# A written TensorE order for the second attention of a four-layer decode kernel

## Chip, cores and metric

The kernel runs on one core of one Trainium2 chip. The metric is the device time of one execution in microseconds. The time before is the median of five runs, 185.16 us (183.58 to 186.29). The profiled execution is a further run.

## The reference

Two kinds of layer alternate, attention and GLU, each used twice with the same weights and the same K and V caches:

```python
x = x + _A_ref(_layernorm(x), A_k_cache, A_v_cache, A_wq, A_wo)   # attention 0
x = x + _B_ref(_layernorm(x), B_w_gate, B_w_up, B_w_down)         # GLU 0
x = x + _A_ref(_layernorm(x), A_k_cache, A_v_cache, A_wq, A_wo)   # attention 2
x = x + _B_ref(_layernorm(x), B_w_gate, B_w_up, B_w_down)         # GLU 1
# _A_ref: q = x @ wq; softmax(q k^T / sqrt(128)) v over the last 2048 positions; @ wo
# _B_ref: (sigmoid(x @ w_gate) * (x @ w_up)) @ w_down
```

The batch is 4, one new position each, D = 512, 32 query heads on 8 KV heads of 128, F = 1792, all in bf16.

## The kernel before

Both attentions walk over the 8 KV heads; one head (all four batches) is a unit, named 0.0 to 0.7 in the first attention and 2.0 to 2.7 in the second. The second takes the heads in reverse, 7 down to 0. A unit consists of: q spread to block form (`qx` on TensorE, L706, and its copy `qe` on ScalarE, L711), the scores S (4 mask matmuls L733 and 16 score matmuls L740), the maximum over them (DVE, L748 to L760), exp (ScalarE, L763), P permuted on TensorE (`pp`, L772), copied (L774) and transposed by DVE into `ebuf` (L779), P times V (PV), the sums of P and their reciprocal, and WO, the product with that head's rows of wo, summed over all units.

In the first attention DVE also transposes K in place (L718), so the second one finds it ready in SBUF. The second attention uses a wide form of PV (`pv_wide`, L897: 16 matmuls of 512 columns) for units 2.0 to 2.6: the product is transposed (`tv`, L905), reduced (`rd`, L910), shifted, added and scaled (`sh`, `ad`, `av`, L912 to L917) on DVE, turned back by two small matmuls (`tr`, L927), copied (`oc`, L933) and multiplied by wo in rows (`wo_wide`, L946). After unit 2.7's PV, which has the narrow form (L817), `wo_back` (L957, L963) brings the row sums of the seven units into the column form that unit 2.7's WO (L977) adds to. Then come the addition to x, the layer norm, the gate and up projections of GLU 1 (L1053), hT (L1080), x as rows (`xrow`, L1096), and the down projection (L1111).

SBUF holds an arena of 50 slots; 32 hold K, the rest is a pool of tiles of two slots, 1 MB each. All large loads go through SP's queue in one fixed order (L391). A load is given the tile that was released first by the time it is planned, and waits for the last reader of that tile. The order of releases in the program text thus decides which work a load waits for. In the second attention 14 V loads follow the four wq loads; one V tile was kept in SBUF and another one is parked in PSUM ("stash") and brought back by four DVE transposes (L510). Tiles are freed by the parts of q (`q_proj`, L671), by S (its head's K is not needed again), by PV and by WO. Small working buffers of the wide form lie in one of the K tiles of unit 2.0 (`wide_buffers`).

The order on each compute engine comes from a list scheduler, `_schedule` (L86): it keeps an estimate of when each operation could start, from durations in `_TM` (L263), and picks the earliest program place among those startable within a tolerance. SP alone follows program order. Semaphores follow from the dependencies. What `attn` (L986) writes down is: units two ahead in S (`front`), then PV, then `turn` for P two ahead, then WO.

Of the kernel before, what the change touches and what calls it, by code (L numbers as in the profile page):

```python
# [40 lines left out]
class _Plan:  # L41
    def __init__(self):
        self.ops = []
        self.last_w = {}
        self.readers = {}
        self.bank_eng = {}
        self.bank_cur = {}
        self.bank_prev = {}

    def op(self, eng, name, dur, emit, r=(), w=(), banks=(), dma_bytes=0, dma_rate=0.0, after=(), lazy=0.0):  # L50
# [26 lines left out]
        for t in w:  # L77
            self.last_w[t] = o
            self.readers[t] = []
        deps.discard(o)  # L80
# [168 lines left out]
class _SlotPool:  # L249
# [17 lines left out]
    pe_pair=34.0, pe_small=230.0, pe_f32=450.0, pe_row=85.0, pe_sq=300.0,  # L267
# [5 lines left out]
def build(nc, A_x, A_k, A_v, A_wq, A_wo, B_wg, B_wu, B_wd, out, cfg=None):  # L273
# [7 lines left out]
    assert GROUPS == [[0, 1, 2, 3]]  # L281
    N_DMA_SEMS = cfg.get("N_DMA_SEMS", 24)
# [32 lines left out]
    with es:  # L315
# [343 lines left out]
        def q_proj(k, b0, b1, variance):  # L659
            assert b0 == 0 and b1 == NB  # L660
            after = ()
            for n, i in enumerate((0, 1) if k == 0 else (1, 0)):
                qb = OBS[n]
                for c in range(NC):
                    name, o = wq_part(k, c, i)
                    s = need(name)

                    def e_q(pe, c=c, s=s, qb=qb, o=o):
                        last = None
                        for hh in range(4):  # L670
                            last = pe.matmul(ps[32 * hh:32 * hh + NB, qb, :], xn[:, c * NB:(c + 1) * NB],  # L671
                                             tile_ap(s)[:, o + hh * 512:o + (hh + 1) * 512],
                                             start=(c == 0), stop=(c == NC - 1))
                        return last
                    P.op("tensor", "q%d_%d_%d" % (k, i, c), 4 * tm["pe_row"], e_q,
                         r=tok(s) + [("xn",)], w=[("qrow", i)], banks=(qb,), after=after if k else ())
                    done(name)
                if variance is not None:
                    variance()
                    variance = None  # L680
                P.op("vector", "qt%d_%d" % (k, i), c_dve(512),
                     lambda v, qb=qb: v.transpose(  # L682
                         ebuf[:, :], ps[:, qb, :].rearrange("p (x k t) -> p x t k", k=32, t=2)),
                     r=[("qrow", i)], w=[("e", 0), ("e", 1)], banks=(qb,))
                qi = qh[:, i * 64:(i + 1) * 64]
                qc = P.op("vector", "qc%d_%d" % (k, i), c_dve(64),
                     lambda v, qi=qi: v.tensor_tensor(
                         qi.rearrange("p (c b r) -> p c b r", c=4, b=NB),
                         ebuf[:, :].rearrange("p (r c y) -> p c y r", c=4, y=32)[:, :, 0:NB],
                         lnr[:, 0:NB].unsqueeze(1).unsqueeze(3).broadcast_to([128, 4, NB, REP]), ALU.mult),  # L690
                     r=[("e", 0), ("e", 1), ("lnr", 0)], w=[("qh", i)])
                if k and n == 0:
                    fresh.append(qc)
                    after = (qc,)
# [28 lines left out]
        def softmax_unit(tag, hk):  # L723
# [3 lines left out]
            bank, pt = (OBS[0], 2) if u == HKV else (SB[k2], k2)  # L727
            q_unit(tag, hk, k2)

            def e_s(pe):  # L730
# [4 lines left out]
                for cp in range(4):  # L735
# [10 lines left out]
            mk = mxt[:, k2 * 32:(k2 + 1) * 32]  # L746
            P.op("vector", "mx" + tag, c_dve(512),
                 lambda v: v.tensor_reduce(nmax[:, k2:k2 + 1], ps[:, bank, :], AXX, ALU.max),  # L748
                 r=[("pss", pt)], w=[("mx", k2)], banks=(bank,))
            for g in range(2):  # L750
                P.op("vector", "nx%d%s" % (g, tag), tm["dve_small"],
                     lambda v, g=g: v.tensor_copy(nmax[64 * g:64 * g + 64, 4 + k2:5 + k2],  # L752
                                                  nmax[64 - 64 * g:128 - 64 * g, k2:k2 + 1]),
                     r=[("mx", k2)], w=[("nx", k2, g)])
            P.op("vector", "mk" + tag, tm["dve_small"],
                 lambda v: v.scalar_tensor_tensor(mk, nmax[:, 4 + k2:5 + k2].broadcast_to([128, 32]), nmax[:, k2:k2 + 1],
                                                  maskr[:, :], ALU.max, ALU.add),
                 r=[("mx", k2), ("nx", k2, 0), ("nx", k2, 1), ("maskr",)], w=[("mk", k2)])
            P.op("vector", "nm" + tag, tm["dve_small"],
                 lambda v: v.tensor_reduce(nmax[:, 2 + k2:3 + k2], mk, AXX, ALU.max, negate=True, apply_transpose=True),  # L760
                 r=[("mk", k2)], w=[("nm", k2)])
            P.op("scalar", "ex" + tag, c_act(512) + 200.0,
                 lambda a: a.activation(prow[:, :].rearrange("p (m x t) -> p m x t", x=32, t=2),  # L763
                                        ps[:, bank, :].rearrange("p (m t x) -> p m x t", x=32, t=2), ACTF.Exp, bias=nmax[:, 2 + k2:3 + k2], scale=1.0,
                                        accum_out=psm[:, k2:k2 + 1]),
                 r=[("pss", pt)] + [("nm", k2)], w=[("prow",), ("psm", k2)], banks=(bank,))
            return k2

        def turn_p(tag, k2, pb, wide=False):
            ob = OBS[k2]  # L770
# [10 lines left out]
            if wide:  # L781
                sums(tag, k2)
                return
# [22 lines left out]
        def pv_unit(tag, h, k2, tiles):  # L806
            ob = OBS[k2]
            ev = ebuf[:, k2 * 256:(k2 + 1) * 256].bitcast(BF16).rearrange("p (m x t) -> p t m x", x=32, t=2)
            for bp, name in tiles:
# [58 lines left out]
        def sums(tag, k2):  # L868
# [4 lines left out]
            out_ = ps[0:64, WB, k2 * 8:k2 * 8 + 8]  # L873
            P.op("tensor", "sb" + tag, tm["pe_f32"],
                 lambda pe: pe.matmul(out_, rest["mb"], pr, start=True, stop=True),
                 r=[("pr", k2), ("mb",)], w=[("psb", k2)], banks=(WB,))
            P.op("vector", "ri" + tag, c_dve(8) + 60.0, lambda v: v.reciprocal(rv[0:64, :], out_),
                 r=[("psb", k2)], w=[("rinv", k2)], banks=(WB,))
            P.op("vector", "rm" + tag, c_dve(64),
# [5 lines left out]
        def pv_wide(tag, h, k2, tiles):  # L885
# [22 lines left out]
            def e_rd(v):  # L908
# [5 lines left out]
            P.op("vector", "ad" + tag, c_dve(32), lambda v: v.tensor_tensor(o32[0:64, :], o32[0:64, :], osh[0:64, :], ALU.add),  # L914
                 r=[("o32", k2), ("osh", k2)], w=[("o32", k2)])
            P.op("vector", "av" + tag, c_dve(256),
# [4 lines left out]
                 r=[("o32", k2), ("rm", k2)], w=[("av", k2)])  # L921
            q0 = 16 + k2 * 16

            def e_tr(pe):
                last = None
                for bb in range(2):
                    last = pe.matmul(ps[:, WB, q0 + bb * 8:q0 + bb * 8 + 8], av[0:64, bb * 128:(bb + 1) * 128], selm[0:64, :],  # L927
                                     start=True, stop=True)
                return last
            P.op("tensor", "tr" + tag, 2 * tm["pe_pair"], e_tr, r=[("av", k2), ("selm",)], w=[("pst", k2)], banks=(WB,))  # L930
            op = opb[:, k2 * NR:(k2 + 1) * NR]
            P.op("vector", "oc" + tag, c_dve(16),
                 lambda v: v.tensor_copy(op.rearrange("p (m b i) -> p i m b", b=2, i=2),  # L933
                                         ps[:, WB, q0:q0 + 16].rearrange("p (i m b) -> p i m b", i=2, b=2)),
                 r=[("pst", k2)], w=[("opb", k2)], banks=(WB,))
# [16 lines left out]

        def wo_back():
            halves = (ebuf[:, 0:256], prow[:, :].bitcast(F32))
            for n, tk in enumerate(("e", "prow")):
                P.op("scalar", "wr%d" % n, c_act(256),
                     lambda a, n=n: a.copy(halves[n], ps[:, PBS[1], n * 256:(n + 1) * 256]),  # L957
                     r=[("psr",)], w=[(tk, 0) if n == 0 else (tk,)], banks=(PBS[1],))

            def e_b(pe):  # L960
                last = None
                for c in range(NC):
                    last = pe.matmul(ps[:, WB, c * NR:c * NR + NB], halves[c // 2][:, c % 2 * 128:(c % 2 + 1) * 128],  # L963
                                     selw[:, :], start=(c == 0), stop=False, skip_group_check=True)
                return last
            P.op("tensor", "wr", NC * tm["pe_f32"], e_b, r=[("e", 0), ("prow",), ("selw",)], w=[("psw",)], banks=(WB,))
# [19 lines left out]
        def attn(L):  # L986
            hs = list(range(HKV)) if L == 0 else list(range(HKV))[::-1]

            def front(ui):
                h = hs[ui]  # L990
                if L == 0:
                    k_transpose(h)
                k2 = softmax_unit("%d.%d" % (L, ui), h)
                if L == 2:
                    if ui == 0:
                        wide_buffers(4 * h + 2, [o for o in P.ops if o.name == "S2.0"][0])
# [15 lines left out]
            for ui, h in enumerate(hs):  # L1012
# [7 lines left out]
                if ui + 2 < HKV:  # L1020
                    turn(ui + 2)
# [235 lines left out]
```

## Time and profile before

| | |
|---|---|
| median of five runs | 185.16 us |
| profiled execution: its own time, its span | 184.38 us, 182.7 us |
| bytes moved, mean rate over the span | 72.07 MB, 395 GB/s |
| DVE busy | 106.4 us, 58% |
| PE busy (matmuls) | 103.3 us, 57% |
| ACT, POOL busy | 32.1 us, 13.2 us |
| second attention, first q matmul to last WO matmul | 121.2 to 171.5 us |

In the 40 slices of the page each stands for 4.6 us; a digit is the busy share in tenths. The chain of waits follows the end of the program back to what released each step; "SPq" in it is time in which SP was issuing a transfer. In tables of stretches each engine has its busy time and its number of instructions, then the granted TensorE clock, the DMA engines' busy share and GB/s. A time to landing runs from the issue of a transfer to the point at which all 16 DMA engines have reported their part.

### The profile page before, as it was taken

To read this page: it belongs to the slowest core of one execution; us is meant where nothing else is said; L and a number is where in the kernel's file an instruction comes from. 1 tells how busy PE (TensorE), PEld (TensorE's weight loads), DVE (VectorE), ACT (ScalarE), POOL (GpSimd) and SP (SyncE) were. 2 spreads that over 40 slices of the span, in tenths; PEclk is the share of its full clock that TensorE was granted. 3 is DMA by queue.
4 is the path that set the end of the run, shared out by engine and by line. 5 is a ranking of instruction groups with operands and counts; after the bars stand their busy time and mean duration, and the time that the engine had idled before them with its cause. 6 is when DMAs were issued, how large, how long until landed. Compare 5 with 4: busy or idle time off the path is not lost.

```text
span 182.7 us, 3750 instructions
## 1 busy us (share of the span) xinstructions
PE 103.3 (57%) x1588; PEld 54.8 (30%) x1599; DVE 106.4 (58%) x280; ACT 32.1 (18%) x80; POOL 13.2 (7%) x65
## 2 busy tenths in 40 slices
PE   1434425572817408254186566436968769756794
PEld 1002111342413405214146531312323324325632
DVE  6209997659394393744942633212898997945250
ACT  2002032121120202102002001001064333322010
POOL 7000010110010100101001000000001000010000
PEclk9999999999999999999999999999999996968559
DMA  5999999999999999999999999999999999999970
GB/s 200 422 425 423 425 414 419 420 422 420 414 422 418 420 420 416 420 422 425 405 425 414 409 402 417 374 386 383 400 335 423 429 420 420 427 406 406 410 315 12
DMA packets 12305, 72.07 MB, mean 395 GB/s; under 512 B 1145, under 2 KB 1153, under 8 KB 5633
## 3 DMA queue, kind: packets, MB, share of 16 engines
q1 hardware_dynamic: 12280, 71.84, 96.3%
q8 instruction: 12, 0.20, 0.4%
q14 instruction: 5, 0.03, 0.0%
q10 hardware_dynamic: 8, 0.00, 0.0%
HBM read 71.83 MB, written 0.00 MB: 393 GB/s over the span
## 4 chain that ended last, share of the span: by engine, by line
DMA 44%; DVE 22%; PE 17%; SPq 10%; issue 3%; ACT 3%; POOL 0%; ACTq 0%
DMA arena<-in_A_v_cache_dram 23%; DMA arena<-in_B_w_down_dram 11%; SPq L391 10%; DVE arena L718 9%; PE ps L740 6%; DMA arena<-in_A_wq_dram 5%; DMA arena<-in_B_w_up_dram 5%; DVE nmax L748 3%; PE ps L733 2%; ACT prow L763 2%; PE ps L817 2%; PE ps L671 2%; DVE ps L500 1%; DVE nmax L752 1%; PE ps L1111 1%
## 5 line engine op out<-in xcount | busy, mean ns | idle before, releaser
L718 DVE STREAM_TRANSPOSE arena<-arena 128x1024 f32<-128x1024 f32 x32 | 37.0, 1204 | 0.0
L740 PE MATMUL ps<-arena,qbd 128*32 128x512 bf16 x256 | 25.2, 528 | 0.0
L817 PE MATMUL ps<-ebuf,arena 128*128 128x8 bf16 x576 | 17.7, 168 | 10.7 <-DMA arena<-in_A_v_cache_dram 5.7
L733 PE MATMUL ps<-msk_m,msk_s 128*32 128x512 bf16 x64 | 8.6, 528 | 22.2 <-DVE arena L718 21.6
L817 PEld LDWEIGHTS ps<-ebuf,arena 128*128 128x128 bf16 x576 | 16.7, 103 | 13.0 <-DMA arena<-in_A_v_cache_dram 6.8
L748 DVE TENSOR_REDUCE nmax<-ps 128x1 f32<-128x512 f32 x16 | 10.9, 680 | 16.3 <-PE ps L740 16.3
L763 ACT ACTIVATE prow<-ps,nmax 128x512 bf16<-128x512 f32 x16 | 11.0, 687 | 34.4 <-DVE nmax L760 33.6
L711 ACT CAST qbd<-ps 128x256 bf16<-128x256 f32 x16 | 5.9, 372 | 47.8 <-PE ps L740 34.9
L671 PE MATMUL ps<-arena,xn 128*4 128x512 bf16 x64 | 8.4, 606 | 8.5 <-DMA arena<-in_A_wq_dram 7.5
L774 ACT CAST prow<-ps 128x512 bf16<-128x512 f32 x16 | 9.4, 585 | 13.4 <-PE ps L772 5.4
L740 PEld LDWEIGHTS ps<-arena,qbd 128*32 128x32 bf16 x256 | 8.6, 122 | 10.4 <-issue 8.0
L682 DVE STREAM_TRANSPOSE ebuf<-ps 128x512 f32<-128x512 f32 x4 | 2.9, 716 | 13.0 <-PE ps L671 12.9
L897 PE MATMUL ps<-arena,ebuf 128*32 128x512 bf16 x112 | 8.9, 446 | 2.2 <-DMA arena<-in_A_v_cache_dram 1.5
L733 PEld LDWEIGHTS ps<-msk_m,msk_s 128*32 128x32 bf16 x64 | 1.8, 98 | 24.0 <-DVE arena L718 18.8
L648 ACT ACTIVATE lnv<-ps 128x4 f32<-128x4 f32 x4 | 0.7, 173 | 44.0 <-PE ps L644 44.0
L1053 PE MATMUL ps<-arena,xn 128*4 128x448 bf16 x64 | 6.8, 564 | 2.4 <-DMA arena<-in_B_w_up_dram 1.7
L786 POOL CAST s<-psm 128x1 bf16<-128x1 f32 x9 | 1.7, 187 | 88.0 <-ACT prow L763 88.0
L706 PE MATMUL ps<-qh,eyew 32*128 32x64 bf16 x64 | 5.5, 217 | 3.2 <-ACT qbd L711 1.9
L779 DVE STREAM_TRANSPOSE ebuf<-prow 128x256 f32<-128x256 f32 x16 | 6.8, 426 | 0.9 <-ACT prow L774 0.6
L905 DVE STREAM_TRANSPOSE arena<-ps 128x512 f32<-128x512 f32 x7 | 4.9, 702 | 3.4 <-PE ps L897 3.4
L825 DVE TENSOR_TENSOR onb<-ps,rinv 128x16 bf16<-128x16 f32 x9 | 1.7, 184 | 8.4 <-PE ps L817 8.4
L977 PE MATMUL ps<-onp,arena 128*128 128x16 bf16 x144 | 5.2, 175 | 2.1 <-DVE onp L840 2.1
(104 smaller groups left out, 123.7 us busy)
## 6 DMA issues: line engine op xcount, KB each, us to landing
arena<-in_A_v_cache_dram SPq DMA_DIRECT2D x30, 1024.0 KB, 22.7
arena<-in_A_k_cache_dram SPq DMA_DIRECT2D x16, 1024.0 KB, 25.1
arena<-in_A_wq_dram SPq DMA_DIRECT2D x8, 1024.0 KB, 9.3
arena<-in_A_wo_dram SPq DMA_DIRECT2D x4, 1024.0 KB, 24.9
arena<-in_B_w_gate_dram SPq DMA_DIRECT2D x4, 896.0 KB, 16.6
arena<-in_B_w_up_dram SPq DMA_DIRECT2D x4, 896.0 KB, 16.5
arena<-in_B_w_down_dram SPq DMA_DIRECT2D x2, 1024.0 KB, 13.2
arena<-in_B_w_down_dram SPq DMA_DIRECT2D x1, 768.0 KB, 7.4
```

Of the source, the lines that this page charges most:

```text
L391: o = P.op("sync", name, 0.0, lambda e, dst=dst, src=src: e.dma_start(dst, src), r=r, w=w, dma_bytes=nbytes, dma_rate=tm[rate])
L671: last = pe.matmul(ps[32 * hh:32 * hh + NB, qb, :], xn[:, c * NB:(c + 1) * NB], tile_ap(s)[:, o + hh * 512:o + (hh + 1) * 512], start=(c = ...
L718: P.op("vector", "T%d_%d" % (h, t), c_dve(1024), lambda v, v32=v32: v.transpose(v32, v32), r=[("slot", 4 * h + t)], w=[("slot", 4 * h + t)])
L733: last = pe.matmul(ps[32 * gi:32 * gi + 32, bank, :], msk_s[:, :], msk_m[:, :].unsqueeze(1).broadcast_to([128, 256, 2]), start=True, stop= ...
L740: last = pe.matmul(ps[32 * gi:32 * gi + 32, bank, :], qbd[:, q0:q0 + 32], kt[:, cp // 2, cp % 2, jh * NJ:(jh + 1) * NJ, :], start=False, s ...
L748: lambda v: v.tensor_reduce(nmax[:, k2:k2 + 1], ps[:, bank, :], AXX, ALU.max),
L763: lambda a: a.activation(prow[:, :].rearrange("p (m x t) -> p m x t", x=32, t=2), ps[:, bank, :].rearrange("p (m t x) -> p m x t", x=32, t ...
L774: P.op("scalar", "pc" + tag, c_act(512), lambda a: a.copy(prow[:, :], ps[:, pb, :]), r=[("ppb", pb)], w=[("prow",)], banks=(pb,))
L779: P.op("vector", "pt" + tag, c_dve(256), lambda v: v.transpose(et, prow[:, :].bitcast(F32)), r=[("prow",)], w=[("e", k2)])
L817: last = pe.matmul(ps[:, ob, bp * 8:bp * 8 + 8], src[:, j * 128:(j + 1) * 128], ev[:, j % 2, j % 16 // 2, x0:x0 + 8], start=(j == 0), stop ...
L897: last = pe.matmul(ps[32 * g:32 * g + 32, ob, :], ew[:, g, mq, t], src.rearrange("p (m t d) -> p t m d", t=2, d=128)[:, t], start=(n == 0) ...
L1053: last = pe.matmul(ps[32 * g:32 * g + NB, OBS[n], 0:NF], xn[:, c * NB:(c + 1) * NB], tile_ap(s)[:, o:o + NF], start=(c == 0), stop=(c == N ...
```

## The change

1. In the second half of the program (`P.chain`) each TensorE operation depends on the one before it, so that TensorE runs in program order there. The first half is still scheduled; `pe_pair` and `pe_row` in `_TM` become 30 and 62.
2. `q_proj` is cut up. In the second attention the variance of the layer norm stands after two of the four parts of the first q half. S2.0 follows that half directly, ahead of the other half of q, whose first two parts come before S2.1 and its last two after.
3. Every unit's S, 2.0 too, releases both its K tiles. The wide buffers move into the last wq tile, which is therefore kept. The stash is brought back after the first V load of the second attention instead of after the second.
4. In a unit, the order is PV of u, P of u+1, S of u+3, sums of u+1, q of u+4, WO of u-1, `tr` of u. S2.1 gets another PSUM bank, and the sums of 2.0 too.
5. `rm`, `ad` and `av` go from DVE to POOL, `oc` from DVE to ScalarE.
6. WO of 2.5 comes before PV of 2.6. `wo_back`, now one copy of 512 columns into a `tv` buffer, comes before the PV of 2.7. WO of 2.6 then takes the column form in 16 narrow matmuls (`wo_compact`), between the two V tiles of 2.7.
7. `xrow` moves from behind the up projection to a place ahead of its last eight matmuls.

```diff
+        if eng == "tensor":
+            if self.chain:
+                deps.add(self.last_t)
+            self.last_t = o
...
-    pe_pair=34.0, pe_small=230.0, pe_f32=450.0, pe_row=85.0, pe_sq=300.0,
+    pe_pair=30.0, pe_small=230.0, pe_f32=450.0, pe_row=62.0, pe_sq=300.0,
...
+        def q_second(variance):
+            q_mms(1, 1, OBS[0], (0, 1))
+            variance()
+            q_mms(1, 1, OBS[0], (2, 3), True)
+            fresh.append(q_turn(1, 1, OBS[0]))
+            done(wq_part(1, NC - 1, 1)[0])
...
-            bank, pt = (OBS[0], 2) if u == HKV else (SB[k2], k2)
+            bank, pt = {HKV: (OBS[0], 2), HKV + 1: (WB, 3)}.get(u, (SB[k2], k2))
...
-            P.op("vector", "av" + tag, c_dve(256),
+            P.op("gpsimd", "av" + tag, 500.0,
...
+        def wo_compact(tag, h, op, k2):
+            name = ("wo", h // 2)
+            s = need(name)
+            o = h % 2 * REP * D
+
+            def e_wo(pe):
+                last = None
+                for m in range(REP):
+                    for c in range(NC):
+                        last = pe.matmul(ps[:, WB, c * NR:c * NR + NB],
+                                         tile_ap(s)[:, o + m * D + c * 128:o + m * D + (c + 1) * 128],
+                                         op[:, m * NB:(m + 1) * NB], start=False, stop=False, skip_group_check=True)
+                return last
...
+            qx(0)
+            score(0)
+            q_mms(1, 0, OBS[1], (0, 1))
+            qx(1)
+            score(1)
+            s = need(wq_part(1, NC - 1, 0)[0])
+            left[wq_part(1, NC - 1, 0)[0]] += 1
+            q_mms(1, 0, OBS[1], (2, 3))
+            wide_buffers(s, P.ops[-1])
+            q_turn(1, 0, OBS[1])
+            qx(2)
+            soft(0)
+            turn(0)
+            soft(1)
+            sum_up(0)
+            score(2)
+            qx(3)
...
+            for u in range(NW):
+                if u == NW - 1:
+                    wo(u - 1)
+                op[u] = pv_wide(tag(u), hs[u], u % 2, v_tiles[(2, hs[u])])
+                turn(u + 1)
+                score(u + 3)
+                soft(u + 2)
+                if u == NW - 1:
+                    wo_back()
+                sum_up(u + 1)
+                qx(u + 4)
+                if 0 < u < NW - 1:
+                    wo(u - 1)
+                if u < NW - 1:
+                    op[u] = late.pop(("tr", tag(u)))()
...
+                    if n and c == 2 and last:
+                        x_rows()
...
-                    if n_v == 2:
+                    if n_v == cfg.get("ST", 1):
```

Here NW is 7, HKV is 8, `score(u)` plans S and releases the K tiles, `soft(u)` the maximum and exp, `turn(u)` P, and `sum_up(u)` the sums.

## Prediction

> **What bounds the kernel now.** I read the 40 slices of the page first, then its chain, then stretches of 2 us where the slices sag, then single DMA issues with their time to landing.
>
> ```profile
> PEclk9999999999999999999999999999999996968559
> DMA  5999999999999999999999999999999999999970
> GB/s 200 422 425 423 425 414 419 420 422 420 414 422 418 420 420 416 420 422 425 405 425 414 409 402 417 374 386 383 400 335 423 429 420 420 427 406 406 410 315 12
> q8 instruction: 12, 0.20, 0.4%
> DMA 44%; DVE 22%; PE 17%; SPq 10%; issue 3%; ACT 3%; POOL 0%; ACTq 0%
> ```
>
> The DMA engines are full from the second slice to the third from last, at about 420 GB/s: the kernel is a stream of 71.84 MB, and arithmetic matters where it delays a load or follows the last one. Only slices 26 to 30 (114 to 137 us) sag. The same place finer; the last two columns are the DMA share and GB/s:
>
> ```profile
> 126.00:128.00 2.00, 1.77 (x20) 0.76 (x24) 0.48 (x2) 0.37 (x1) 0.00 (x0) 1.00 1.04 424
> 130.00:132.00 2.00, 2.00 (x28) 0.63 (x28) 1.22 (x4) 0.37 (x1) 0.00 (x1) 1.00 0.96 406
> 132.00:134.00 2.00, 1.54 (x28) 0.62 (x24) 1.86 (x7) 0.82 (x2) 0.00 (x0) 1.00 0.86 283
> 134.00:136.00 2.00, 0.61 (x10) 0.45 (x7) 1.86 (x9) 1.23 (x4) 0.31 (x1) 1.00 1.06 393
> 136.00:138.00 2.00, 1.97 (x27) 0.85 (x31) 1.64 (x7) 1.34 (x3) 0.31 (x1) 1.00 0.92 365
> ```
>
> Against 422, the stretches from 130 to 138 miss (16 + 139 + 29 + 57) x 2 = 482 KB, 1.1 us of stream. The hole belongs to a late issue. Timeline of SP, then its wait:
>
> ```profile
> 122.31 3.04 SPq L391 DMA_DIRECT2D arena<-in_A_v_cache_dram  x2
> 131.00 11.25 SPq L391 DMA_DIRECT2D arena<-in_A_v_cache_dram  x12
> SPq L391 <- PE ps L671: 5.6, 1, 5.6
> DMA to landing us min/median/max: 7.0/7.0/7.0
> ```
>
> The second V loads V1 and V2 go out at 122.3 and 124.8, V3 at 131.0, because its slot is freed by the last eight q matmuls (L671). Asked singly, V1 and V2 take 9.7 us each (landing at 132.0 and 134.5) and V3 7.0 (138.0, the line above): 3.5 us after V2 where full-speed neighbours come 2.5 apart. The shortest time to landing of any load, the first of all, is 4.8 us; so V3's last part waited about 2.2 us behind V2. Hence most DMA engines ran dry while the last one did not, and a landing is that of the last one. The end, from the chain in order of time:
>
> ```profile
> 157.99 20.14 DMA arena<-in_B_w_down_dram
> 178.13 0.04 issue
> 178.18 1.23 PE ps L1111 x15
> 180.06 0.40 PE ps L1111 x4
> 180.49 0.42 DVE ebuf L1121
> ```
>
> The last w_down matmuls wait for landings at 178.13, 179.4 and 180.0. hT, their other operand, is ready at 177.92 (L1080 starts at 177.70 and takes 0.22). So transfers and arithmetic meet within 0.2 us: an end earlier by more needs both.
>
> [...] the 16 score matmuls of S2.0 take 1.92 us at 127.76, those of S2.1 1.11 at 131.00, though PEclk shows full speed there. [...]
>
> **The change part by part.** The order of instructions decides which release feeds which load.
>
> *Start of the second attention.* Before: first half of q, S2.0 after two of the four remaining q parts, V1 and V2 into the first two freed wq slots, the stash into the third, V3 into the fourth. After: V1 into the first wq slot, stash into the second, V2 and V3 into the two K slots of S2.0, V4 into the third wq slot; the fourth becomes the wide buffers, which used to lie in a K slot. So V2 now waits for S2.0. S2.0's last matmul ended at 129.68 (127.76 + 1.92). After, the variance matmul (0.59) stands before the second q pair, so qh need not wait for it: the transpose ends at 125.53, the scaling 0.27 later at 125.8 instead of 126.09, and the eight q matmuls (1.02) no longer sit ahead of the scores, which began at 127.33 on that account instead of 127.05 when qbd was there. S2.0 ends at 129.68 - 0.28 - 0.27 = 129.1. V2 goes out at 129.2 instead of 124.8, V3 and V4 at about 129.8 and 130.3 instead of 131.0 and 131.6. From V3 on loads are issued 1.2 us earlier, but V2 4.4 later.
>
> What this does to the stream can only be bounded. Good end: V2 still lands on time (129.2 + 4.8 = 134.0, before 134.5), as the last engine is still busy with V1 until 132.0, and V3 follows 2.5 later, the extra 1.0 us of its interval gone: -1.0. Bad end: engines run dry one transfer earlier, 129.2 + 2.5 = 131.7 stands in place of 131.0: +0.7. I take the middle, -0.15. After that the queue is deep in both (landings 22 to 25 us after issue for the last V loads), so S three units ahead, which frees K slots earlier, buys nothing[...].
>
> *Per unit.* DVE loses rm 0.18, ad 0.18, av 0.42, oc 0.14 = 0.9 us of about 4.3; POOL gains rm, ad, av. [...] ACT gains oc, about 0.2. All is hidden under the stream: a unit needs two V loads, 4.97 us, and PE's work in it is PV 1.05, P 0.39, S 1.5, sums 0.28, q 0.28, WO 0.39, turn 0.20 = 4.1. With the order written out, PE waits at tr for av: [...] P, S, sums, q and WO stand between, 2.8. [...]
>
> *Tail.* Before (timeline of PE):
>
> ```profile
> 169.21 1.01 PE L963 MATMUL ps<-msks,ebuf 128*128 128x4 f32 x4 [0.51 <-ACT prow L957]
> 170.94 0.57 PE L977 MATMUL ps<-onp,arena 128*128 128x16 bf16 x16
> 173.19 1.66 PE L1053 MATMUL ps<-arena,xn 128*4 128x448 bf16 x16 [0.36 <-DVE xT L632]
> 175.31 1.66 PE L1053 MATMUL ps<-arena,xn 128*4 128x448 bf16 x16
> 176.75 1.06 PE L1096 MATMUL ps<-prow,xT 128*4 128x128 f32 x8
> ```
>
> After: PV2.6 (161.93 to 163.83, it waits for V), P 0.6, the turned-back sums 1.86, sums 0.27: PV2.7's first half starts at 166.4, ends at 167.3; tr 0.2, oc 0.2 and handovers, WO2.6 in 16 narrow matmuls 0.6: 168.4; second half 0.95: 169.4; then as before oe, pm, oq, WO: 170.9. Before that stood at 171.51, so the gate projection starts 0.6 earlier, at 172.6. But xrow (1.06, with its handover 1.2) now stands ahead of the last eight w_up matmuls instead of behind them. Net: hT 0.6 later, 178.5, w_down from 178.7 instead of 178.18: +0.5. That is with TensorE at half clock, as PEclk shows over the last slices; at full clock the sums and projections halve, hT is ready 1 us sooner, and the landings decide: 0. I take half, +0.25.
>
> Sum: -0.15 + 0.25 = +0.1 us on the profiled execution (span 182.7, its time 184.38, 1.7 outside the span). The median, 185.16, is 0.8 above that execution; 185.16 + 0.1 is 185.3.
>
> **Rivals.** *The hole closes* (0.19): the stream recovers the 1.1 us, and the last landing's lag shrinks too. The page's instruction row is 12 packets on single engines, 0.4% of 16 x 182.7 us or 1 us each; one that hits the last engine delays every landing (the V load issued at 139.5 takes 22.3, landing at 161.8, and that at 141.6 lands at 166.6, although a cadence of 2.49 from 138.0 would give 160.4 and 165.4). If another engine is hit, 1 us more: 185.16 - 2.1 = 183.1. For: the tail work is then earlier by the same. Against: V2 is later than before.
>
> *Slower* (0.21): xrow in the tail. If TensorE is cold and turning back gains nothing, the gate projection starts at 173.2 as before and hT is 1.2 late; its price is 1 us for each us that the projection starts after 172.0 (178.13 less 6.1 of work from there to w_down: 2.1 to the first w_up matmul, half of w_up 0.83, xrow 1.2, the other half 0.83, hT 0.95, handover 0.2). With V loads 0.7 late as well it starts at 173.9: +1.9, 187.1.
>
> *The change does little because the stream decides* is my forecast (0.6): ends -1.0 to +1.3, so 184.2 to 186.5.
>
> **How the numbers follow.** One per cent is 1.85 us, about what a measurement of this kernel can tell from no change. The forecast's cases all lie within it. Faster by over 1% is the first rival, 0.19; slower the second, 0.21; same 0.6. The range reaches into both until a tenth is left on each side: 183.1 to 187.2.
>
> **What would show it.** V2 issued near 129.2, and a dip in GB/s near 130 to 134 instead of 132 to 138, show the first step; no dip says the good end. Landings of w_down at 178 to 180 show that the stream decides; if w_down matmuls wait for hT instead, the tail does. A wait of PE on POOL at tr in every unit, or V loads landing unwaited-for, would break the hidden step. A last landing before 178.5 would make the forecast wrong.

## The result, and the profile after

| | before | after |
|---|---|---|
| median, same session | 184.17 us (71 runs, 182.84 to 186.56) | 184.48 us (36 runs, 183.61 to 185.85) |
| profiled execution: its own time, span | 184.38, 182.7 | 184.39, 182.7 |
| last landing of w_down | 180.02 | 179.15 |
| last w_down matmul | 180.45 | 180.47 |

The ratio is 1.0018, 95% interval 1.0002 to 1.0034: 0.3 us slower, where +0.1 was forecast, and far within one per cent. The forecast of 185.3 us was counted from a median of five runs, 185.16; 71 runs put the kernel before at 184.17, so only the difference can be compared. Runs over 1.5% above the fastest of their kernel are left out of all ratios here (16 of 22 with S two ahead, 10 of 22 and 6 of 14 with the stash later, 7 of 22 without the written order, at most 4 in each of the other versions), so a ratio can differ from that of two medians.

The page of the changed kernel, the same lines as were shown of the kernel before:

```profile
PEclk9999999999999999999999999999999999996555
DMA  5999999999999999999999999999799999999980
GB/s 193 427 425 429 420 417 421 414 423 418 416 422 423 414 422 416 418 422 425 405 426 418 406 402 413 370 389 394 296 414 423 425 422 425 416 411 411 410 330 10
DMA 44%; DVE 24%; PE 22%; SPq 3%; issue 3%; ACT 3%; DVEq 0%; ACTq 0%
```

The kernel is still a stream. Its sag is one slice (296 GB/s), and TensorE's clock (PEclk) now stays at half to the end (0.50 in every stretch of 2 us from 168 to 182; in the kernel before 0.85 from 178 to 180 and 1.00 from 180 to 182). The nines of PEclk up to 130 us stand for no record: the first record of the clock starts at 130.82 in the trace of the kernel before and at 135.49 in that of the changed one. In the kernel before the single score matmuls take 628 to 634 ns up to 129.7 us and 379 to 409 from 131.0 to 148.1. PV2.6, whose matmuls also have 512 columns, takes 583 to 634 ns each under a recorded 0.50 (161.93). By these durations TensorE ran at half clock ahead of the first record. The stretches of 2 us, with DMA share and GB/s last:

```profile
128.00:130.00 2.00, 2.00 (x20) 0.41 (x12) 1.34 (x3) 0.00 (x0) 0.00 (x0) 1.00 0.75 315
130.00:132.00 2.00, 1.54 (x20) 0.68 (x20) 0.77 (x5) 1.15 (x3) 0.00 (x0) 1.00 0.61 229
132.00:134.00 2.00, 2.00 (x20) 0.41 (x12) 0.69 (x1) 0.00 (x0) 0.00 (x0) 1.00 1.03 426
136.00:138.00 2.00, 2.00 (x33) 0.72 (x25) 1.64 (x8) 1.04 (x3) 0.59 (x2) 1.00 1.03 434
```

The hole lies 2 us earlier and is deeper than before (0.61 against 0.86), behind V2, which is issued at 129.3. Then the end, from the chain in order of time, and the same place on TensorE's timeline:

```profile
158.10 19.18 DMA arena<-in_B_w_down_dram
177.28 0.04 issue
177.32 3.17 PE ps L1212 x28
180.51 0.42 DVE ebuf L1222
```

```profile
170.06 1.67 PE L1172 MATMUL ps<-arena,xn 128*4 128x448 bf16 x16 [0.36 <-DVE xT L639]
172.58 0.92 PE L1172 MATMUL ps<-arena,xn 128*4 128x448 bf16 x8 [0.33 <-DMA arena<-in_B_w_up_dram]
173.28 1.06 PE L1153 MATMUL ps<-prow,xT 128*4 128x128 f32 x8
174.84 0.92 PE L1172 MATMUL ps<-arena,xn 128*4 128x448 bf16 x8 [0.49 <-DMA arena<-in_B_w_up_dram]
177.32 3.15 PE L1212 MATMUL ps<-arena,hT 128*4 128x256 bf16 x28 [1.57 <-DMA arena<-in_B_w_down_dram]
```

Before, the w_down matmuls came in pieces that waited for landings, 2.27 us in all, and ended 0.43 after the last landing. Now they are one piece of 3.15 us that waits for nothing after its start and ends 1.32 after the last landing. The gate projection starts 3.1 us earlier (170.06 against 173.19), the transfers land 0.87 earlier, and 0.89 is given back in 28 matmuls at half clock (PEclk 0.50 from 176 to 182). In these two profiles the 0.87 is owed to one interval: the eleventh of the 14 V loads lands at 158.35 against 157.82, later than before, and the twelfth 2.48 after it (160.83) against 4.02 (161.84).

### The profile page after: what moved, and what is told of

The parts are those of the page before. It is cut to its first block, busy times and chain, and to the rows that moved or that the text cites. A ratio compares the mean times of both kernels' runs of the same rounds, so it can differ in the third digit from the quotient of the medians.

```text
span 182.7 us, 3781 instructions
## 1 busy us (share of the span) xinstructions
PE 102.5 (56%) x1600; PEld 54.7 (30%) x1611; DVE 102.0 (56%) x252; ACT 32.8 (18%) x86; POOL 21.1 (12%) x86
## 4 chain that ended last, share of the span: by engine, by line
DMA 44%; DVE 24%; PE 22%; SPq 3%; issue 3%; ACT 3%; DVEq 0%; ACTq 0%
DMA arena<-in_A_v_cache_dram 23%; DMA arena<-in_B_w_down_dram 10%; DVE arena L731 9%; PE ps L756 7%; DMA arena<-in_A_wq_dram 5%; DMA arena<-in_B_w_up_dram 5%; DVE nmax L765 4%; SPq L398 3%; PE ps L923 3%; PE ps L749 3%; DVE arena L931 2%; PE ps L1212 2%; PE ps L842 2%; DVE ebuf L800 2%; PE ps L674 2%
## 5 line engine op out<-in xcount | busy, mean ns | idle before, releaser
L756 PE MATMUL ps<-arena,qbd 128*32 128x512 bf16 x256 | 25.9, 540 | 0.0
L923 PE MATMUL ps<-arena,ebuf 128*32 128x512 bf16 x112 | 7.3, 381 | 0.0
```

Source lines behind the costliest of these rows:

```text
L756: last = pe.matmul(ps[32 * gi:32 * gi + 32, bank, :], qbd[:, q0:q0 + 32], kt[:, cp // 2, cp % 2, jh * NJ:(jh + 1) * NJ, :], start=False, s ...
L923: last = pe.matmul(ps[32 * g:32 * g + 32, ob, :], ew[:, g, mq, t], src.rearrange("p (m t d) -> p t m d", t=2, d=128)[:, t], start=(n == 0) ...
```

## Experiments

Each ran in five rounds beside the kernel before on the same chip, four kernels to a session. In the sessions the kernel before had medians of 184.23, 184.40 and 184.58. The ratios are to it.

### xrow back behind the up projection

```diff
-                    if n and c == 2 and last:
-                        x_rows()
...
+                x_rows()          # ahead of w_down
```

> The changed kernel with one part undone: the residual rows (xrow) are again multiplied behind the last eight w_up matmuls, just ahead of w_down, instead of between the two halves of w_up. Theory clock (the changed kernel's gain in the stream and in the tail is lost because its w_down matmuls run at half clock, 3.15 us for 28 in place of 2.27): xrow fills the gap ahead of w_down again (174.84 to 176.82 without a gap, then at most 0.5 us of waiting), TensorE is granted full clock near 178.6 as before, the matmuls that are left then take half as long and the end follows the last landing by 0.4 us instead of 1.3: 0.5 to 0.9 us faster than the changed kernel. Theory stream (the time is set by when the loads land, and the tail is hidden): no change, within 0.2 us. Theory order (the written order and the products on GpSimd cost time in every unit): no change, within 0.2 us.

Measured 184.62 us, ratio 1.0033 (1.0012 to 1.0054): no gain. Timeline of TensorE:

```profile
172.83 0.92 PE L1170 MATMUL ps<-arena,xn 128*4 128x448 bf16 x8 [0.33 <-DMA arena<-in_B_w_up_dram]
175.04 0.92 PE L1170 MATMUL ps<-arena,xn 128*4 128x448 bf16 x8 [1.29 <-DMA arena<-in_B_w_up_dram]
177.57 2.96 PE L1211 MATMUL ps<-arena,hT 128*4 128x256 bf16 x28 [0.76 <-DMA arena<-in_B_w_down_dram]
```

xrow filled one gap and opened another, 1.29 us in the middle of w_up. The granted clock was 0.50 up to 180 and rose only in the last slice of the page (178.1 to 182.7, digit 7), too late. So the place of xrow is not the cause: the early tail leaves TensorE waiting for w_up and w_down with xrow in either place.

### Extra matmuls in the gaps

```diff
+                    for _ in range(times):
+                        last_ = pe.matmul(ps[:, SB[0], :], perm[:, :], permo[:, :], start=True, stop=True)
...
+                        fill_pe("fill0", 1)      # behind xrow
...
+                fill_pe("fill1", 3)              # behind w_up
```

> The changed kernel with four extra matmuls of 128x512 that nobody reads: one behind xrow, three behind the second half of w_up, in the gaps where TensorE waits for transfers. They add work and can't shorten anything but by the clock. Theory clock: TensorE is busy almost without a gap from 172.6 on, full clock is granted by 176.5 to 177.5, w_down then waits for its landings only, and the end is 0.7 to 0.9 us earlier than that of the changed kernel. Theory stream and theory order: 0 to 0.3 us slower, as only work is added.

Measured 184.03 us, ratio 0.9996 (0.9968 to 1.0023), 0.6 below the kernel of the last experiment in the same session. Its last landing is at 179.50, later than the changed kernel's, and its last w_down matmul at 179.93, earlier. A second version has one more extra matmul ahead of the first half of w_up:

> The changed kernel with the four extra matmuls ahead of w_down and a fifth between the variance and the first half of w_up, so that no gap over 0.2 us is left between the gate projection and the last wait. Theory clock: full clock is granted in time in every run, w_down follows its landings, and the time is that of the kernel with four extra matmuls (184.0) or up to 0.2 us less: 0.4 to 0.7 us below the changed kernel, and at or below the kernel before. Theory stream: 0 to 0.3 us above the changed kernel.

Measured 184.19 us against 184.58 in its session, ratio 0.9971 (0.9951 to 0.9992). This is the one version whose interval lies below 1, and it doesn't touch the changed kernel's (1.0002 to 1.0034, from another session). Its timeline:

```profile
174.50 0.39 PE L1163 MATMUL ps<-permo,perm 128*128 128x512 bf16 x1
175.28 0.55 PE L1183 MATMUL ps<-arena,xn 128*4 128x448 bf16 x8 [0.39 <-DMA arena<-in_B_w_up_dram]
175.76 0.82 PE L1163 MATMUL ps<-permo,perm 128*128 128x512 bf16 x3
177.76 1.04 PE L1224 MATMUL ps<-arena,hT 128*4 128x256 bf16 x16 [1.18 <-DMA arena<-in_B_w_down_dram]
178.97 1.02 PE L1224 MATMUL ps<-arena,hT 128*4 128x256 bf16 x12 [0.17 <-DMA arena<-in_B_w_down_dram]
```

w_down is in pieces again, the second waiting for its landing, and ends at 179.99, 0.43 after the last one (179.56). The stretch ahead of it shows the clock, the third number from the end, first of this kernel, then of the changed one:

```profile
176.00:178.00 2.00, 0.82 (x9) 0.28 (x9) 0.75 (x2) 0.00 (x0) 0.00 (x0) 1.00 0.75 294
```

```profile
176.00:178.00 2.00, 0.68 (x8) 0.43 (x10) 0.67 (x2) 0.00 (x0) 0.00 (x0) 0.50 0.63 246
```

Work was only added, and the time fell: the half clock at w_down is shown to be a loss of the changed kernel, 0.4 to 0.9 us by the ratios (1.0018 against 0.9996 and 0.9971).

### The same on the kernel before: xrow ahead, extra matmuls, no xrow

```diff
+                    if n and c == 2 and last:
+                        x_rows()          # first kernel: ahead of the last eight w_up matmuls
...
+                P.op("tensor", "fill1", 400.0, e_f, ...)   # second: two extra behind xrow
...
-                P.op("tensor", "xrow", 1200.0, e_x, ...)   # third: without xrow
```

> The kernel before with one part of the change alone: xrow is multiplied between the two halves of w_up instead of behind them. Theory clock: hT comes 1 us later (near 179.0) and TensorE idles ahead of w_down, so that its matmuls run at half clock for longer: the end is 0.4 to 1.8 us later than that of the kernel before, 1.2 as the middle. Theory stream: 0, the landings decide (last one at 180.0, half of w_down's work already done). Theory order: 0.

> The kernel before with two extra matmuls of 128x512 that nobody reads, between xrow and w_down. Theory clock: the kernel before was granted full clock at 178.6 us anyway, shortly after the first w_down matmuls, so the extra work buys nothing there: -0.2 to +0.4 us. If extra matmuls shortened it by 0.5 us as they did the changed kernel, the gain of the extra matmuls would have nothing to do with what the change did to the clock.

> The kernel before without xrow: the output lacks the residual rows, so there is 1.06 us less for TensorE to do ahead of w_down and nothing else changes. Theory clock: w_up ends near 177.0, TensorE idles until 178.2, is not granted full clock at 178.6, and the 28 matmuls take 3.0 to 3.15 us instead of 2.27 or less: 0.4 to 0.9 us slower than the kernel before although it does less. Theory stream or tail: 0, or faster by up to 0.2 us.

Measured 184.91 (ratio 1.0044, 1.0017 to 1.0072), 183.88 (0.9995, 0.9965 to 1.0025) and 184.68 us (1.0003, 0.9977 to 1.0028). The time of the first is as expected, at the low end, but the reason expected isn't seen: its profiled execution is a quick one (183.79 us), in which w_down waits for hT (it starts at 178.06), the matmuls ahead run without a gap, and w_down takes 1.81 us, with the PEclk digit 9 in the last slice. Why its median is higher isn't shown. The second shows no gain, as expected, but its times decide little: the interval doesn't exclude a gain of 0.5 us, and its median is 0.52 below that of its session. The profiles say more: w_down ends 0.43 after the last landing in the kernel before and in this one (180.74 against 180.31), as in the changed kernel with extra matmuls, and 1.32 after it in the changed kernel alone. The third shows the loss in its profile, 1.42 us of waiting and then 3.15 us for w_down:

```profile
177.85 3.15 PE L1097 MATMUL ps<-arena,hT 128*4 128x256 bf16 x28 [1.42 <-DMA arena<-in_B_w_down_dram]
```

It runs at half clock (PEclk 0.50 from 172 to 180, 3.15 us) and ends at 181.00, 1.32 after its last landing; but its time is unchanged, so the 0.4 to 0.9 expected did not come. With xrow gone, hT is also free of 1.06 us of work ahead of w_down, which helps the runs in which the tail is late; whether that balances it isn't shown.

### The stash one V load later, alone and with the extra matmuls

```diff
-                    if n_v == cfg.get("ST", 1):
+                    if n_v == cfg.get("ST", 2):
```

> The changed kernel with the stashed tile brought back after the second V load of the second attention instead of after the first, so that V1 and V2 both go into slots of wq, as in the kernel before, and neither waits for the scores S2.0. Theory stream: the 2 us hole at 129 to 132 us (share of busy DMA 0.61) becomes that of the kernel before or less, as V2 is issued near 124.5 instead of 129.3, V3 still near 129.9: landings 0.3 to 0.6 us earlier and the time 0.3 to 0.6 us shorter than that of the changed kernel. Theory clock: the landings come earlier as well, but w_down still runs at half clock and starts 0.3 to 0.6 us earlier only if its first tile lands earlier: 0.2 to 0.5 us. These two are told apart by the other kernels; this one shows what the place of V2 is worth. If the lost bytes are made up elsewhere: 0.

> The changed kernel with the stash brought back one V load later and, in addition, the four extra matmuls that nobody reads ahead of w_down. With the stash later alone, the stream had no hole at all between 126 and 138 us (DMA share 1.01 to 1.03), the last landing came at 179.08 as in the changed kernel (179.15), but PV2.0 began 0.9 us later (the four transposes of the stash stand in the softmax of S2.0 and S2.1), hT came at 177.3, and 28 cold matmuls followed it. Theory slowest engine (the hole makes only those DMA engines wait that are ahead; the last landing belongs to the one that never waits): closing the hole buys nothing even with TensorE warm, so this kernel is not faster than the one with the extra matmuls alone (184.0), rather 0 to 1 us slower through the late units. Theory stream (the hole costs its missing bytes): with the cold tail mended, 0.5 to 1 us faster than the one with the extra matmuls alone.

Measured 185.64 us (ratio 1.0037, 1.0008 to 1.0066) and 186.42 (1.0023, 0.9977 to 1.0068): not faster, and by the medians 1.4 and 2.0 us slower than the kernel before in their sessions. Stretches of the first:

```profile
128.00:130.00 2.00, 2.00 (x22) 0.46 (x14) 0.78 (x2) 0.00 (x0) 0.00 (x0) 1.00 1.03 432
130.00:132.00 2.00, 1.54 (x32) 0.80 (x32) 1.97 (x4) 0.37 (x1) 0.00 (x0) 1.00 1.01 426
132.00:134.00 2.00, 0.74 (x16) 0.18 (x5) 1.76 (x6) 0.37 (x1) 0.24 (x1) 1.00 1.00 414
170.00:180.00 10.00, 7.82 (x70) 4.03 (x72) 3.64 (x13) 0.72 (x4) 0.00 (x0) 0.50 0.66 265
```

and the last stretch of the changed kernel:

```profile
170.00:180.00 10.00, 7.54 (x68) 3.32 (x70) 2.81 (x8) 0.72 (x4) 0.00 (x0) 0.50 0.75 302
```

The hole is closed: 432, 426, 414 GB/s. The engines finish sooner on the average (0.66 busy over the last 10 us against 0.75), and yet the last landing is at 179.08 against 179.15. A landing is that of the last DMA engine; the hole, then, made mostly the others wait. That is inferred, as no view names the engine of a packet, but the V loads agree: the second lands at 134.71 behind the hole and at 134.42 without it, the fourth at 140.76 and 140.46. The stash's four transposes (2.66 us of DVE from 129.22) stand in the first softmaxes: PV2.0 starts at 137.75 instead of 136.82, the units stay behind, and w_down now waits for hT, starts at 177.40 and runs at half clock (3.15 us). Over all profiles the last landing is at 179.4 to 180.3 with the load order of before (four kernels, mean 179.86), 178.9 to 179.7 with that of after (eight, 179.35), 179.1 with the stash later (two). By these the hole is worth about 0.3 us (an estimate: the two lie within the range of the eight), not its missing bytes ((107 + 193) x 2 = 600 KB against 422 GB/s in the changed kernel, 1.4 us). The kernel with the extra matmuls does not decide between its two theories: in its profiled execution, a long one (186.46 us), the last landing is at 179.05 but hT comes at 180.69, so the late units set its end, by more than the 0 to 1 us expected.

### Parts of a unit: products on VectorE, S two ahead, no written order

```diff
-            P.op("gpsimd", "av" + tag, 500.0,           # rm and ad likewise
+            P.op("vector", "av" + tag, c_dve(256),
...
-                score(u + 3)
+                score(u + 2)
...
-        P.chain = True
+        P.chain = False
```

> The changed kernel with the three products of every wide unit (rm, ad, av) back on VectorE; the copy of the turned-back outputs stays on ScalarE. Theory hidden (a unit's work lies under the two V loads that it needs, 4.97 us, and the units run at 3.93): no change, within 0.3 us. Theory order (TensorE waits some 0.4 us per unit, and 1.66 us in unit 5, for the products on GpSimd): the products take 0.18, 0.18 and 0.42 us on VectorE against 0.29, 0.24 and 0.67 on GpSimd, so the wait is 0.4 us shorter per unit, unless VectorE is busy with the next softmax just then: 0.3 to 1 us faster if the units decide, 0.3 to 0.8 slower if the products now hold up the softmax.

> The changed kernel with the scores S two units ahead instead of three. Theory hidden ([...] a unit's work lies under its two V loads): no change, within 0.3 us. Theory order (the score matmuls three units ahead are what TensorE does while it would otherwise wait for the softmax): the pace of the units rises above 3.93 us, PV2.6 begins after 161.5 and the gate projection after 171; the time is 0 to 1 us longer, as the tail has some 2 us to spare before it is late.

> The changed kernel with the order of TensorE in the second attention left to the scheduler, as in the kernel before: all other parts of the change stay, but the scheduler moves S and P against PV and puts xrow ahead of the layer norm. Theory hidden: the units stay under the stream, and the time is within 0.4 us of the changed kernel. Theory order: the units become uneven, PV2.6 begins later than 161.5, and the time is 0.5 us longer or more. With xrow gone from ahead of w_up, TensorE is no warmer at w_down than in the changed kernel, so no gain is expected.

In the second kernel the spreading of q (`qx`) moves one unit later together with S. Measured 184.48 us (ratio 1.0023, 0.9998 to 1.0047), 188.32 (184.58 to 191.04; ratio 1.0079, 1.0037 to 1.0120) and 186.67 (1.0078, 1.0053 to 1.0104). The first fits: no change. Units take 4.17 us instead of 3.93, PV2.6 starts 1.9 us later (162.86), and the tail swallows it: hT comes at 178.34, and w_down takes 1.69 us, as at full clock. The other two are the largest effects of the study, and the theory that fell in both is "hidden", which was mine. Against the changed kernel's 1.0018 each costs 0.6%, 1.1 us. Without the written order PV2.6 starts at 163.56, at half clock (1.90 us against 1.05), the gate projection at 173.81, and w_down waits for hT (178.54) and takes 3.06 us. With S two ahead the profiled execution is one of the longest (190.72 us, span 189.0): the first two units take 6.1 us each, the later ones 4.79, PV2.6 starts at 168.82, the gate projection at 177.9. The waits of TensorE from 140 to 170 us (sum, times, longest), then DVE and POOL in one of its units:

```profile
PE ps L957 <- DVE arena L903: 7.9, 6, 1.5
```

```profile
156.49 0.65 DVE L765 TENSOR_REDUCE nmax<-ps 128x1 f32<-128x512 f32 x1
157.18 0.33 DVE L769 COPY nmax<-nmax 64x1 f32<-64x1 f32 x2
157.54 0.25 DVE L773 SCALAR_TENSOR_TENSOR mxt<-nmax,maskr 128x32 f32<-128x32 f32 x1
157.83 0.21 DVE L777 TRANSPOSE_TENSOR_REDUCE nmax<-mxt 128x1 f32<-128x32 f32 x1
157.96 0.16 DVE L903 RECIPROCAL arena<-ps 64x8 f32<-64x8 f32 x1
```

```profile
156.50 0.67 POOL L943 TENSOR_TENSOR arena<-arena 64x256 bf16<-64x256 f32 x1
```

`tr` (L957) starts at 158.27. Its operand av was ready at 157.17; it waits for the reciprocal of the next unit's sums, which lies in the same PSUM bank (WB), and on DVE the reciprocal stands behind the whole maximum of S, which came late. With S three ahead the reciprocal comes straight after the first reduction (152.32), av at 152.42, and `tr` at 152.65 waits 0.42. These waits are 3.3 us more than those at `tr` in the changed kernel (4.6 in six). They are less than half of the 7.9 us by which PV2.6 is later: TensorE also has one S more to do behind PV2.0, and ran at half clock for a part of this time: the 16 score matmuls took 1.92 us at 131.76 and 1.88 at 144.94, against 1.12 at 150.34, and PV2.0 took 1.90 (136.55), against 1.05 for the PV at 148.81. How the rest divides between these two isn't shown.

### The tail undone

```diff
-                if u == NW - 1:
-                    wo_back()
...
+            wo(u - 1)       # wide, behind the last V tile
+            wo_back()
+            wo_unit(tag(u), hs[u], ov, u % 2, False, True)
```

> The changed kernel with one part undone: unit 6 goes through the wide output projection as the other units, and the sums of the wide projection are turned back behind the last V tile instead of ahead of unit 7. The gate projection then starts near 172.4 us instead of 170.06. Theory tail hidden (the end is the last landing of w_down plus what is left to multiply): hT comes near 178.3 instead of 176.7, but TensorE is busy without a gap ahead of it and is granted full clock: no change, between -0.3 and +0.5 us. Theory tail decides (the turning back between V tiles earns its 2.3 us): 1 to 2 us slower than the changed kernel.

Measured 184.59 us, ratio 0.9995 (0.9965 to 1.0025): no change.

```profile
172.30 1.66 PE L1173 MATMUL ps<-arena,xn 128*4 128x448 bf16 x16 [0.35 <-DVE xT L639]
178.02 1.69 PE L1213 MATMUL ps<-arena,hT 128*4 128x256 bf16 x28 [1.10 <-DVE hT L1200]
```

The gate projection starts 2.24 us later than in the changed kernel, hT comes about 1.2 later, and w_down ends 0.8 earlier (179.71): 0.26 of it because the last landing is earlier (178.89), the rest because its w_down matmuls take 1.69 us instead of 3.15, as at full clock, TensorE having run from 172.30 to 176.92 without a gap.

## Why the prediction was right or wrong

**The number**, +0.1 forecast and +0.3 measured (interval 0.0 to 0.6), came close by luck: it is a sum of terms of which several were off and cancelled. Two sums in the working are slightly off as well, without weight: 163.83 + 0.6 + 1.86 + 0.27 is 166.56, not 166.4, and the worst ends of the two terms, +0.7 and +0.5, make +1.2, not +1.3.

**The stream decides** was right up to the start of w_down: both kernels wait for its landing. The step that failed comes behind that. I priced two cases, half clock with a late hT (+0.5) and full clock, where "hT is ready 1 us sooner, and the landings decide: 0". What came was a third: hT was ready 1.2 us sooner (176.71 against 177.92) at half clock, and the landings did not decide the end, as w_down ended 1.32 us after the last of them, 0.89 more than before.

**The start of the second attention**: S2.0 at 129.1 (measured 129.27), V2 issued at 129.2, V3 and V4 at 129.8 and 130.3 (129.32, 129.90, 130.55) were right; the dip came at 128 to 132, 2 us ahead of the forecast. Its price, -0.15 as the middle of -1.0 and +0.7, was not. What failed is the reading "482 KB, 1.1 us of stream" under it: by the landings those bytes were missing on DMA engines that were ahead, as inferred above, and with the hole wholly closed the last landing moved by 0.07 us in that kernel, 0.3 over all. The long interval ahead of V3 was also not V3's late issue: with V3 issued 1.8 us earlier and no hole it is 3.5 us (134.42 to 137.97), as long as before. A 16 KB instruction packet falls at 134.38 there, at 132.93 before (0.98 us long), and at 138.58 after (0.99), where V4 is the late one (137.23 to 140.76). That the packet is the cause agrees with these traces; no run moved the packet alone.

**The tail** is the mis-sized term. The gate projection was forecast at 172.6 and came at 170.06, as PV2.6 started at 160.96 instead of 161.93 and ran at full clock (1.05 us instead of 1.90). The 1.2 us of xrow cost nothing, being covered by the wait for w_up. Where I had +0.25 the profiles show 0.89, w_down at 3.15 us instead of 2.27, behind transfers that landed 0.87 earlier. I priced half clock for what stands ahead of w_down and not for w_down itself: the step "w_down from 178.7 instead of 178.18" moved its start and left its duration alone. I did not ask which gaps the earlier tail would open.

**Per unit**: on POOL av takes 0.66 to 0.67 us, rm 0.29 and ad 0.24, and av came 2.5 us after PV. My forecast for POOL was an estimate that rested on no trace of these products. The wait at `tr`, forecast as hidden, came in every unit, 0.4 us in three of six and up to 1.66, since the work ahead of it took 2.35 us and not 2.8; five of the waits end with the reciprocal and one, the longest, with POOL. "Hidden under 4.97" was too simple: PV2.1 starts 6.3 us behind its V tile (141.01 against 134.71), the lag shrinks by 1.2 a unit, and PV2.6 starts as its tile has landed (160.96 against 160.83). A unit of 4.79 us gains only 0.2 on 4.97 and does not catch up.

**S three ahead buys nothing** failed. I looked at the loads, and there SP issued from 146.3 to 163.5 us with pauses of 0.04 in the kernel before, so no slot held it up; in this order of TensorE and DVE it is worth 0.86 us in each of the later units of one long execution, 0.6% (1.1 us) by the ratios, and some 3.4 us of median (3.7 above the kernel before of its session, against 0.3).

**The rivals.** The landings were earlier, as in the first, and not by a closed hole: the late landing at 161.8, which that rival names, has no counterpart in the profile of the changed kernel. xrow as the slower one was not seen: the tail starts 2 us before the point from which it would decide.

So earlier landings and an earlier tail met a new loss, the clock at the end. The loss is shown. That the change makes landings earlier (about 0.5 us by the profiles) is not: one profile a kernel stands behind each, their ranges overlap, and up to the eleventh V load the means of the two load orders are alike (158.59 before, 158.49 after).

## What to carry to other kernels

Where an end waits for transfers, price the matmuls that follow the last landing at the clock that they will run at; here an early tail in front of a transfer left the 28 of w_down at 3.15 us instead of 2.27, and matmuls that nobody reads cost less than the gaps that they filled (ratios of 0.9996 and 0.9971 against 1.0018). The mean DMA share is not the landing: look at intervals between landings, and don't take a hole's missing bytes for lost time; here 1.4 us of them moved the landings by 0.3. Whether work is hidden under a stream depends on where it starts, not on its pace alone.

## What the runs showed of the hardware

In the records of the clock TensorE was granted 0.50 or 1.00. In the kernel before it was 0.50 from 151.30 to 154.71, from 161.54 to 164.95 and from 168.37 to 178.61, and 1.00 in the rest from 130.82 on; in the changed kernel 1.00 from 135.49 to 166.21 and 0.50 from there to the end. The 16 matmuls of PV took 1.90 us at 0.50 (PV2.6 of the kernel before, 161.93) and 1.05 at 1.00 (136.03).

TensorE's busy time ahead of w_down, its clock, and the time of the 28 w_down matmuls:

| | busy us in 172 to 174, 174 to 176, 176 to 178 | PEclk in 176 to 178, 178 to 180 | w_down, us |
|---|---|---|---|
| before | 1.40, 2.00, 1.82 | 0.50, 0.85 | 2.27 |
| changed | 1.67, 1.26, 0.68 | 0.50, 0.50 | 3.15 |
| changed, xrow back | 1.41, 0.96, 1.24 | 0.50, 0.50 | 2.96 |
| before, no xrow | 1.64, 2.00, 0.58 | 0.50, 0.50 | 3.15 |
| changed, four extra matmuls | 2.00, 2.00, 1.29 | 1.00, 1.00 | 1.04 + 1.01 |
| changed, five extra matmuls | 1.62, 1.61, 0.82 | 1.00, 1.00 | 1.04 + 1.02 |

A gap alone does not tell whether the clock falls: in the changed kernel TensorE was busy 1.18 us from 156 to 158 and 0.60 from 158 to 160, and the clock stayed at 1.00 up to 166.21; in the kernel before it was busy 1.08 us from 148 to 150, and the clock fell at 151.30. What decides is not shown.

Around the hole of the kernel before (DMA share 0.86 from 132 to 134) some packets of 8 KB took 0.76 to 0.86 us instead of 0.31 (132.6 to 134.2). It is no rule for holes: around the deeper one of the changed kernel (130 to 132) the longest took 0.69.
